# Induced attention and a leaky feed-forward net on one core: deferred softmax sums of the first group and a new order of the first 48 blocks

## The chip, the core and the metric

The kernel runs on one core of one Trainium2 chip. The metric is device time in microseconds (us) for one launch; before the change it is 1496.11 us, the median of 3 runs (1496.09 to 1496.35). Engines are called by the profile's names: PE (TensorE), DVE (VectorE), ACT (ScalarE), POOL (GpSimd), SP (SyncE, which here gives out nearly all DMA transfers).

## What is computed

`x` has 4 batches of 12480 tokens with 128 channels; `inducing` has 32 rows. First the 32 rows attend to all tokens of a batch (this gives `h`), then all tokens attend to `h`, then a feed-forward net with a leaky activation follows.

```python
def mab(q, kv):
    s = scale * (q @ kv.transpose(0, 2, 1))
    s = s - s.max(-1, keepdims=True)
    a = np.exp(s)
    a /= a.sum(-1, keepdims=True) + 1e-09
    return a @ kv
h = mab(I, x)
attn = mab(x, h)
g = np.maximum(0.01 * (attn @ w_in), attn @ w_in)
out = g @ w_out
```

## The kernel before, in words

The tokens of a batch are split into six groups of 2048 tokens (0 to 5) and a remainder of 192 (RG). A group makes four tiles of 512 tokens; there are 98 tiles. The net's inner width of 2048 is cut into 16 pieces of 128, so a tile is 16 blocks. A block (lines 697 to 760) is one product `ph` (L705: the second attention's weights times `h` times `w_in`, both in high and low halves), its positive part `ghi` on ACT (L718), the rest `glo` on DVE (L726) and three products into `po` (L744: `ghi` with `w_hi`, `glo` with `w_hi`, `ghi` with `w_lo`). The linear part of the activation is one more product per tile, with `m2s` (L763). `ph` has three buffers (`LOOK`), so that the product of block u+3 needs the `glo` of block u done. After a tile, DVE transposes `po` to `osb` (L773) and SP stores it in four transfers (L791).

Everything runs through two stages. Up to block 47 the program is written out in the table `ORDER`: each name is a step (function `start`, L822 on), and each engine gets its instructions in that order. Names used below: `W` warm-up products on PE; `T` and `C` transpose a piece of `x` (PE) and copy it; `S` scores, `M` their maxima, `X` and `N` their combination over partitions, `E` exponential, `Y` transpose, `Z` sum, `H` products with `x`, `K` their gathering; `z` and `rz` the sum over partitions and its inverse, `pre` and `K2` the last combination, `hT` the product that turns `h`; `a`, `b`, `o`, `t`, `p` convert a piece of the 64-bit weights (ACT, DVE, DVE, ACT, POOL: L1018 to L1044); `sh`, `sl` split a piece of `w_out` (ACT, POOL); `wt`, `wc`, `wm`, `wd` turn a piece of `w_in`, copy it, multiply it with `w_out` (`w_ps`, L1069) and add it up for `m2s`; `s2`, `y`, `ymx`, `ysub`, `yex`, `ysm`, `ysr`, `ymul`, `yT`, `ah`, `alo` are the second attention's scores and softmax of group 0 and the split of its weights; `rep` and `J` make from it the inputs `A` of tiles 0 and 1 (L1093, L1097), `dA` those of tiles 2 and 3 by transfers; the same names with a 1 are group 1, and `dB` spreads its `ahi` and `alo` into the inputs `A` of tiles 4 to 7, by 16 transfers (L656). `F`, `G`, `L`, `A`, `B` are `ph`, `ghi`, `glo`, the first `po` product and the other two of a block; `os` is a tile's transpose and store. Blocks 0 to 31 alternate between tiles 0 and 1.

From block 48 on a loop (at the end of the kernel function) gives out each block and, between blocks, steps of generators for the next batches, by a count of due work. `first_scores` loads the next batch's `x` in pieces `xc` with three buffers (L248, SP) that DVE transposes to `xT` (L395). The transposes stand in DVE's queue between `glo` of the running blocks. The order of this stage is fixed when the program is built.

```python
if u + LOOK < NT * NF:
    ffn_first(u + LOOK)
ffn_second(u)
```

Of the kernel before, what the change touches and what calls it, by code (L numbers as in the profile page):

```python
# [9 lines left out]
F32 = mybir.dt.float32  # L10
# [10 lines left out]
def induced_attention_then_leaky_ffn(  # L21
# [34 lines left out]
    while N - base >= 4 * TOK:  # L56
# [13 lines left out]
    LOADS = {17: 1, 24: 7}  # L70
    WEIGHTS = [("in", 0), ("out", 0), ("in", 1), ("out", 1), ("in", 2), ("out", 2), ("in", 3), ("out", 3)]
# [3 lines left out]
        W W W W W W W W indT T0.0 W T0.1 W T0.2 W W C0.1a T0.3 W W W C0.2v C0.3a C0.0a S0 T1.0 T1.1 C1.0v  # L75
        T1.2 C1.1a M0 C1.2a T2.0 T1.3 C2.0a T2.1 C1.3a T2.2 C2.1a C2.2v T2.3 S1 C2.3v S2 M1 T3.0 M2 T3.1
        T3.2 C3.0v C3.1a X0 C3.2a T3.3 N0 T4.1 E0 C3.3v T4.0 t0 S3 E2 E1 a0 b0 Y0 C4.1v H0 M3 T4.2 Y1 T4.3
        C4.0a o0 T5.0 C4.3a T5.2 C4.2v p0 C5.0a T5.1 Z1 C5.2a Y2 S4 C5.1a Z2 T5.3 a1 b1 M4 TR.0 t1 wt0 CR.0a
        o1 X1 C5.3a SR a2 b2 p1 N1 H1 MR E3 o2 S5 al1 t2 Z3 H2 a4 b4 p2 M5 wc0 W t4 K0 X2 o4 wt1 E4 wm0 N2
        p4 Y3 E5 Y4 H3 al2 a6 Z4 b6 t6 Z5 H4 o6 wd0 ER p6 wt2 a7 b7 Y5 ZR t7 K1 z o7 H5 wc1 rz p7 wc2 YR pre  # L80
        a5 HR wt3 K2 a3 hT b3 b5 hTc t3 o3 s2 wc3 o5 p3 sh3 hw y wm1 ymx wh t5 ysubv wl p5 yex wd1 hd0 ysm
        sg2 wm2 sh2 ysr sh0 ymulv sh1 s21 yT sl1 wd2 W ah wm3 alov sl0 hd1 rep0 wd3 y1 rep1 sl3 J0 ymx1 J1 F0 F1
        G0 m2 sgR ysub1g dA2 A0 L0 G1 F2 sl2 G2 B0 L1 mh F3 hd2 A1 L2 G3 B1 F4 L3 A2 G4 F5 B2 ml yex1 L4 A3 F6
        G5 B3 dA3 A4 L5 G6 F7 B4 G7 L6 F8 A5 B5 G8 L7 F9 A6 G9 B6 hd3 L8 F10 A7 ysm1 G10 B7 F11 L9 A8 G11 B8
        A9 L10 F12 B9 ysr1 G12 F13 L11 A10 ymul1g G13 B10 L12 A11 B11 A12 L13 F14 B12 G14 yT1 A13 F15 F16
        L14 G15 B13 A14 L15 G16 F17 B14 G17 A15 L16 B15 A16 L17 F18 B16 G18 A17 F19 L18 F20 G19 B17 A18 L19
        G20 B18 F21 A19 L20 G21 F22 B19 L21 G22 A20 F23 B20 G23 L22 A21 F24 B21 L23 G24 F25 A22 G25 B22 L24
        A23 B23 L25 F26 A24 G26 F27 B24 L26 G27 F28 A25 B25 G28 L27 A26 F29 B26 L28 G29 F30 A27 G30 B27 L29
        F31 L30 A28 G31 B28 os0 A29 F32 B29 L31 G32 F33 A30 L32 G33 B30 A31 F34 L33 B31 G34 A32 L34 ah1 F35
        B32 G35 alo1v A33 B33 L35 F36 dB F37 G36 A34 B34 L36 G37 F38 A35 B35 G38 L37 F39 A36 G39 B36 L38 A37  # L90
        F40 B37 L39 G40 A38 F41 L40 F42 G41 B38 A39 L41 G42 B39 F43 A40 L42 G43 B40 F44 os1 yg2 ygR A41 G44 B41 L43
        A42 F45 B42 L44 G45 A43 B43 L45 F46 A44 G46 B44 F47 L46 A45 G47 F48 B45 L47 G48 A46 F49 B46 G49 L48
        A47 F50 B47 L49 G50 L50 os2
# [25 lines left out]
    own = const.tile([P, 4], F32, tag="own", name="own")  # L119
    w_in_sb = const.tile([P, DFF], F32, tag="w_in_sb", name="w_in_sb")  # L120
# [573 lines left out]
    live, accs, fetches = {}, {}, []  # L694
    slots = [
# [72 lines left out]
    def store(t):  # L768
# [4 lines left out]
        nc.vector.transpose(osb[:, :n], po[:, :n])  # L773
        yield HEAVY
        o = 0
        for b, g, js in tiles[t]:
            base, J, K = GROUPS[g]
            n = 32 * K
            for j in js:
                row = b * N + base + j * 32 * K  # L780
                if len(tiles[t]) > 1:
                    dst = out[row : row + n, :].rearrange("(r k) c -> r k c", k=K)
                else:
                    dst = out[row : row + n, :].rearrange("(v r u) c -> r u v c", v=2, u=K // 2)
# [38 lines left out]
    def start(stacking, seconds, chosen):  # L823
# [57 lines left out]
        def peak(g):  # L881
            J, K, rows, w = size(g)
            p, i = step_of[g]
            if ("rd", p) not in V:
                V["rd", p] = small(f"rd{p}", 4 * len(STEPS[p]))
# [4 lines left out]
            rm = small(f"rm{g}")  # L890
            if J < 4:
# [5 lines left out]
            nc.vector.tensor_scalar(  # L897
                out=V["rd", p][:, 4 * i : 4 * i + 4], in0=own, scalar1=rm, scalar2=None, op0=ALU.mult,
                op1=ALU.min, accum_out=small("any"),
            )  # L900
            V["e", g] = e

        def X(p):
            n = 4 * len(STEPS[p])
            V["X", p] = pm = aux_ps("mx_ps")
            nc.tensor.matmul(pm[:, :n], same, V["rd", p], start=True, stop=True)
# [17 lines left out]
        def E(g):  # L924
            J, K, rows, w = size(g)
            V["zg", g] = zg = small(f"zg{g}")
            if J < 4:
# [16 lines left out]
        def Z(g):  # L944
            p, i = step_of[g]
            old, V["z"] = V["z"], small(f"z{g}")
            if i:
                nc.vector.tensor_tensor(out=V["z"], in0=old, in1=V["zg", g], op=ALU.add)
            else:
                nc.vector.tensor_scalar(  # L950
                    out=V["z"], in0=old, scalar1=V["al", p], scalar2=V["zg", g], op0=ALU.mult, op1=ALU.add
                )

# [46 lines left out]
        def pre():  # L1000
            p = len(STEPS) - 1
            V["pre"] = r = sb.tile([P, C], F32, tag="hacc", name="pre", bufs=2)
            nc.vector.tensor_scalar(
                out=r, in0=V["hacc", p - 1], scalar1=V["al", p], scalar2=V["rz"], op0=ALU.mult, op1=ALU.mult
            )
# [139 lines left out]
        def warm():  # L1145
# [7 lines left out]
            "W": warm, "z": z_product, "rz": rz, "pre": pre, "hT": hT_product, "hTc": hT_copy,  # L1153
# [7 lines left out]
        for i, end in enumerate(["", "1"]):  # L1161
# [3 lines left out]
            for name, n in [("ymx", 1), ("ysub", 1), ("yex", 2), ("ysm", 1), ("ysr", 1), ("ymul", 1), ("yT", 3)]:  # L1165
                plain[name + end] = lambda gen=gen, n=n: go(gen, n)
# [35 lines left out]
    with tc.manual_schedule():  # L1202
# [76 lines left out]
```

## Time and profile before

| what | value |
|---|---|
| median of 3 runs | 1496.11 us (1496.09 to 1496.35) |
| the profiled execution: its time, its span | 1496.72 us, 1494.6 us |
| PE busy | 1480.1 us (99%) |
| DVE, ACT, POOL busy | 1265.5 us (85%), 999.6 us (67%), 112.4 us (8%) |
| granted TensorE clock | 0.998 of full speed |
| HBM read, written | 48.94 MB, 25.56 MB |
| first `ph` product | 52.48 us after the span's start |

The profile shows one execution. The span runs from the first to the last instruction of the program; the time of the execution lies 2.1 us above it. Busy time of an engine is a union over its instructions; matmuls are pipelined, so that the start of one after another, and not the length of one, is PE's pace.

### The profile page before, as it was taken

The numbers are of one execution on the slowest core, as the hardware profiler recorded it, in microseconds if no ns is written. First come the engines' busy times: TensorE is split into PE (matmuls) and PEld (weight loads), VectorE is DVE, ScalarE is ACT, GpSimd is POOL, SyncE is SP. The second block draws the span as 40 slices with busy tenths as digits, with TensorE's granted clock in tenths as the row PEclk, the third lists the DMA queues.
The fourth block names the chain that finished last, engine by engine and source line by source line (L and its number), as shares of the span: only waits on it lengthen the run. The fifth ranks groups of instructions, "written<-read, shape, count | busy, mean of one in ns | idle before, by whom it ended". The sixth has DMA issues, their size and how long they took to land.

```text
span 1494.6 us, 22249 instructions
## 1 busy us (share of the span) xinstructions
PE 1480.1 (99%) x7861; PEld 1262.8 (84%) x7861; DVE 1265.5 (85%) x2137; ACT 999.6 (67%) x1748; POOL 112.4 (8%) x182
## 2 busy tenths in 40 slices
PE   8999999999999999999999999999999999999998
PEld 6788888888889888888888888888888898888887
DVE  6888898879898898789899898798888888888886
ACT  5766666666676666676676666676766766666665
POOL 1300100000100100000010100010100000000000
PEclk9999999999999999999999999999999999999999
DMA  8127446335444432243533531231212212212211
GB/s 285 44 56 137 82 78 158 61 59 95 82 103 82 111 82 50 43 96 69 110 69 68 135 67 19 43 73 20 50 34 38 43 25 49 43 24 48 41 26 22
DMA packets 402079, 105.23 MB, mean 70 GB/s; under 512 B 372624, under 2 KB 375088, under 8 KB 401968
## 3 DMA queue, kind: packets, MB, share of 16 engines
q1 hardware_dynamic: 401920, 103.80, 33.7%
q8 instruction: 62, 1.02, 0.3%
q14 instruction: 49, 0.40, 0.1%
q10 hardware_dynamic: 48, 0.02, 0.0%
HBM read 48.94 MB, written 25.56 MB: 50 GB/s over the span
## 4 chain that ended last, share of the span: by engine, by line
PE 95%; DMA 2%; DVE 1%; SPq 1%; ACT 0%; issue 0%; POOL 0%; DVEq 0%; ACTq 0%
PE po L744 67%; PE ph L705 23%; PE s_ps L262 3%; PE po L763 1%; PE h_ps L438 1%; DMA xr<-in_x_dram 1%; DMA raw<-in_moe_w_out_dram 0%; DMA raw<-in_moe_w_in_dram 0%; SPq L248 0%; SPq L833 0%; PE w_ps L1069 0%; DVE glo L726 0%; ACT ghi L718 0%; DMA xc<-in_x_dram 0%; PE hw_ps L545 0%
## 5 line engine op out<-in xcount | busy, mean ns | idle before, releaser
L718 ACT ACTIVATE ghi<-ph 128x512 fp32r<-128x512 f32 (+1 forms) x1568 | 929.5, 595 | 463.7 <-PE ph L705 458.5
L726 DVE SCALAR_TENSOR_TENSOR glo<-ph,ghi 128x512 fp32r<-128x512 f32 (+1 forms) x1568 | 1041.9, 679 | 185.4 <-ACT ghi L718 163.0
L705 PE MATMUL ph<-A,hws 128*128 128x512 f32 (+1 forms) x1600 | 596.6, 377 | 1.6 <-DVE glo L726 1.3
L744 PE MATMUL po<-ghi,w_hi 128*128 128x512 f32 (+1 forms) x1568 | 593.7, 379 | 0.0
L744 PE MATMUL po<-glo,w_hi 128*128 128x512 f32 (+1 forms) x1568 | 593.1, 378 | 0.0
L744 PE MATMUL po<-ghi,w_lo 128*128 128x512 f32 (+1 forms) x1568 | 593.0, 378 | 0.0
L705 PEld LDWEIGHTS ph<-A,hws 128*128 128x128 f32 x1600 | 301.9, 189 | 59.3 <-DVE glo L726 5.6
L744 PEld LDWEIGHTS po<-glo,w_hi 128*128 128x128 f32 x1568 | 296.4, 189 | 41.9 <-DVE glo L726 0.7
L744 PEld LDWEIGHTS po<-ghi,w_lo 128*128 128x128 f32 x1568 | 296.3, 189 | 41.1
L744 PEld LDWEIGHTS po<-ghi,w_hi 128*128 128x128 f32 x1568 | 296.4, 189 | 39.9 <-ACT ghi L718 0.2
L773 DVE STREAM_TRANSPOSE osb<-po 128x512 f32<-128x512 f32 (+1 forms) x98 | 68.8, 702 | 1.5 <-PE po L763 1.5
L644 POOL TENSOR_TENSOR alo<-aT,ahi 128x512 fp32r<-128x512 f32 x22 | 28.1, 1279 | 486.1 <-ACT ahi L639 451.4
L395 DVE STREAM_TRANSPOSE xT<-xc 128x512 f32<-128x512 f32 x72 | 50.5, 701 | 1.6 <-DMA xc<-in_x_dram 1.6
L597 POOL TENSOR_TENSOR y<-y,mx 128x512 f32<-128x512 f32 x23 | 24.2, 1051 | 278.5 <-DVE mx L595 218.7
L612 POOL TENSOR_TENSOR y<-y,sm 128x512 f32<-128x512 f32 x23 | 24.1, 1049 | 189.1 <-DVE sm L610 159.9
L763 PE MATMUL po<-A,m2s 128*128 128x512 f32 (+1 forms) x100 | 37.1, 374 | 0.0
L355 DVE STREAM_TRANSPOSE y<-s_ps 128x512 f32<-128x512 f32 x22 | 15.7, 715 | 10.8 <-PE s_ps L262 9.2
L262 PE MATMUL s_ps<-xT,indT 128*32 128x512 f32 x192 | 24.2, 595 | 0.5 <-ACT xT L871 0.5
L262 PE MATMUL s_ps<-xT,hT 128*32 128x512 f32 x192 | 24.0, 597 | 0.4 <-ACT hT L1013 0.4
L763 PEld LDWEIGHTS po<-A,m2s 128*128 128x128 f32 x100 | 18.9, 189 | 2.6
L280 DVE TENSOR_SCALAR_CACHE_REDUCE e<-s_ps 128x512 f32<-128x512 f32 x18 | 12.4, 690 | 8.3 <-PE s_ps L262 7.5
L438 PE MATMUL h_ps<-xr,ay 128*32 128x128 f32 x576 | 17.6, 274 | 0.0
(152 smaller groups left out, 376.6 us busy)
## 6 DMA issues: line engine op xcount, KB each, us to landing
xr<-in_x_dram SPq DMA_DIRECT2D x96, 256.0 KB, 5.1
out_dram<-osb SPq DMA_DIRECT2D x384, 64.0 KB, 2.2
xc<-in_x_dram SPq DMA_DIRECT2D x288, 64.0 KB, 2.7
A<-ahi SPq DMA_DIRECT2D x188, 64.0 KB, 2.0
A<-alo SPq DMA_DIRECT2D x188, 64.0 KB, 2.0
hws<-hilo SPq DMA_DIRECT2D x64, 64.0 KB, 2.0
raw<-in_moe_w_in_dram SPq DMA_DIRECT2D x4, 512.0 KB, 7.8
raw<-in_moe_w_out_dram SPq DMA_DIRECT2D x4, 512.0 KB, 8.3
```

The costliest lines, as they stand in the source:

```text
L262: nc.tensor.matmul(dst, lhsT, rhs, start=True, stop=True)
L395: nc.vector.transpose(t[:, j, :], blk.rearrange("p n c -> p (n c)"))
L438: nc.tensor.matmul(hp[32 * k : 32 * k + 32, :C], ay[:rows, 4 * q + k, :], xb[:rows, k, :], start=(i == 0 and q == 0), stop=(last[k] == i a ...
L597: engines[0].tensor_tensor(out=yv, in0=yv, in1=mx[:rows, :K].unsqueeze(2).broadcast_to([rows, K, M]), op=ALU.subtract,)
L612: engines[1].tensor_tensor(out=yv, in0=yv, in1=smv.unsqueeze(2).broadcast_to([rows, K, M]), op=ALU.mult)
L644: (engine or nc.gpsimd).tensor_tensor(out=alo[sl], in0=aT.pop((b, g))[: 32 * J, :], in1=ahi[sl].bitcast(F32), op=ALU.subtract,)
L705: nc.tensor.matmul(ph[:, o : o + w], hw[b][1][:, f * P : (f + 1) * P], woven(A4[t][:, o : o + w], t), start=True, stop=True,)
L718: nc.scalar.activation(halves(ghi[:, :n], t)[1], live[u][2], AF.Relu)
L726: nc.vector.scalar_tensor_tensor(out=halves(glo[:, :n], t)[1], in0=ph, scalar=0.0, in1=halves(ghi[:, :n], t)[1].bitcast(F32), op0=ALU.max, ...
L744: nc.tensor.matmul(accs[t][:, :n], w[:, f, :], woven(r[:, :n], t), start=(f == 0 and w is w_hi and r is live[u][0]), stop=False,)
L763: nc.tensor.matmul(accs[t][:, o : o + w], hw[b][2], woven(a4[:, o : o + w], t), start=False, stop=(o + w == n),)
L773: nc.vector.transpose(osb[:, :n], po[:, :n])
```

## The change

Four things change. (1) The second softmax of group 0 leaves its weights undivided: the sums and their inverse are made later, spread over partitions by a product (`sc`), copied (`sq`), and POOL multiplies the transposed output `osb` of tiles 0 to 3 with them before the store. The split reads the turned weights in another order of tokens, and the store of these tiles uses plain rows. (2) The last combination of `h` no longer takes the inverse sum: `pre` is gone, and ACT scales the matrix `same` of the product `hT` by it (`sr`). Maxima and sums of a step are combined once per step and not once per group. (3) The weights arrive in another order, all of `w_in` first, and the first of them after 21 pieces of `x` and not 18. (4) The table `ORDER` is new.

```diff
-    LOADS = {17: 1, 24: 7}
-    WEIGHTS = [("in", 0), ("out", 0), ("in", 1), ("out", 1), ("in", 2), ("out", 2), ("in", 3), ("out", 3)]
+    LOADS = {20: 1, 24: 7}
+    WEIGHTS = [("in", 0), ("in", 1), ("in", 2), ("in", 3), ("out", 0), ("out", 1), ("out", 2), ("out", 3)]
...
-        A42 F45 B42 L44 G45 A43 B43 L45 F46 A44 G46 B44 F47 L46 A45 G47 F48 B45 L47 G48 A46 F49 B46 G49 L48
-        A47 F50 B47 L49 G50 L50 os2
+        A45 B45 G47 L47 G48 A46 L48 F49 F50 G49 L49 G50 ymul1g os1 yT1 ah1 alo1v dB B46 A47 B47 os2 L50
+        ygR
...
         nc.vector.transpose(osb[:, :n], po[:, :n])
+        if t < 4:
+            turned = osb.rearrange("p (k c) -> p k c", c=32)
+            nc.gpsimd.tensor_tensor(
+                out=turned, in0=turned,
+                in1=token_scale[0][:, t, :].unsqueeze(2).broadcast_to([P, 16, 32]), op=ALU.mult,
+            )
...
         def X(p):
+            nc.vector.tensor_tensor(
+                out=rd.rearrange("p (n j) -> p n j", j=4),
+                in0=V["rm", p].unsqueeze(2).broadcast_to([P, n, 4]),
+                in1=own.unsqueeze(1).broadcast_to([P, n, 4]),
+                op=ALU.mult,
+            )
...
-                    out=new, in0=hp, scalar=V["rz"], in1=V["pre"], op0=ALU.mult, op1=ALU.add
+                    out=new, in0=V["hacc", p - 1], scalar=V["al", p], in1=hp, op0=ALU.mult, op1=ALU.add
...
-        def pre():
+        def scaled():
+            V["samez"] = r = sb.tile([P, P], F32, tag="samez", name="samez", bufs=1)
+            nc.scalar.mul(r, same, V["rz"])
...
-            nc.tensor.matmul(ph[:, :P], V["hs"], same, start=True, stop=True)
+            nc.tensor.matmul(ph[:, :P], V["hs"], V["samez"], start=True, stop=True)
...
+        def scales():
+            nc.vector.tensor_tensor(out=apart, ...
+            nc.tensor.matmul(
+                pc[:, :64], same, apart.rearrange("p t k -> p (t k)"), start=True, stop=True
+            )
+        def scales_copy():
+            nc.scalar.copy(r.rearrange("p t k -> p (t k)"), V.pop("sc")[:, :64])
...
         def split_high():
-            nc.scalar.copy(ahi, aT[0, 0])
+            nc.scalar.copy(ahi.rearrange("p (a b i) -> p a b i", a=2, b=16), turned_view(aT[0, 0]))
```

How the order moves, at three places.

PE between the copy of `hT` and the first blocks, before: after the scores of group 2 (`s_ps`) a `w_ps` group, the scores of group 1, and two more `w_ps` groups, the last behind warm-up products.

```order
L1069 MATMUL w_ps<-wraw,winT 128x128 x4
L262 MATMUL s_ps<-xT,hT 32x512 x4
L1148 LDWEIGHTS ident
L1148 MATMUL warm_ps<-ident 128x256
L1148 LDWEIGHTS ident
L1148 MATMUL warm_ps<-ident 128x256
L1069 MATMUL w_ps<-wraw,winT 128x128 x4
L1093 MATMUL a_ps<-ahi,pick 128x512
L1093 MATMUL a_ps<-alo,pick 128x512
L1093 MATMUL a_ps<-ahi,pick 128x512
L1093 MATMUL a_ps<-alo,pick 128x512
L705 MATMUL ph<-A_815,hws 128x512 x2
```

PE at the same place now, from the `a_ps` products on:

```order
L1162 MATMUL a_ps<-ahi,pick 128x512
L1162 MATMUL a_ps<-alo,pick 128x512
L1162 MATMUL a_ps<-ahi,pick 128x512
L1162 MATMUL a_ps<-alo,pick 128x512
L1217 LDWEIGHTS ident
L1217 MATMUL warm_ps<-ident 128x256
L1217 LDWEIGHTS ident
L1217 MATMUL warm_ps<-ident 128x256
L712 MATMUL ph<-A_727,hws 128x512 x3
L1085 MATMUL w_ps<-wraw,winT 128x128 x4
L751 MATMUL po<-ghi,w_hi 128x512
```

One `w_ps` group still stands before `a_ps`; three others, one turn of `w_in` and the product `sc_ps` now stand among the blocks.

DVE at the end of the 48 blocks, before: the transposes of the outputs of tiles 1 and 2 stand eight `glo` apart, and the split `alo` of group 1 twenty rows of work earlier.

```order
L773 STREAM_TRANSPOSE osb<-po 128x512
L726 SCALAR_TENSOR_TENSOR glo<-ph,ghi 128x512 x4
L644 TENSOR_TENSOR alo<-aT,ahi 128x512
L726 SCALAR_TENSOR_TENSOR glo<-ph,ghi 128x512 x8
L773 STREAM_TRANSPOSE osb<-po 128x512
L355 STREAM_TRANSPOSE y<-s_ps 128x512
L355 STREAM_TRANSPOSE yr<-m_ps 96x64
L726 SCALAR_TENSOR_TENSOR glo<-ph,ghi 128x512 x8
L773 STREAM_TRANSPOSE osb<-po 128x512
```

DVE at the same place now:

```order
L733 SCALAR_TENSOR_TENSOR glo<-ph,ghi 128x512 x16
L780 STREAM_TRANSPOSE osb<-po 128x512
L623 STREAM_TRANSPOSE aT<-y 128x512
L646 TENSOR_TENSOR alo<-aT,ahi 128x512
L780 STREAM_TRANSPOSE osb<-po 128x512
L733 SCALAR_TENSOR_TENSOR glo<-ph,ghi 128x512
L357 STREAM_TRANSPOSE yr<-m_ps 96x64
```

The transpose of tile 1's output, the weights' transpose, the split and the transpose of tile 2's output now stand together between the 50th `glo` and the 51st.

SP before, from the store of tile 0 to the first `xc` loads of the next batch (the spread `dB` is 16 transfers to four tiles `A4`, the first two are shown, and the last):

```order
L791 DMA out_0_dram<-osb_1137 256x2x32 x4
L656 DMA A4_1192<-ahi_1175 32x512
L656 DMA A4_1192<-alo_1176 32x512
...
L656 DMA A4_1207<-alo_1176 32x512
L791 DMA out_0_dram<-osb_1279 256x2x32 x4
L791 DMA out_0_dram<-osb_1353 256x2x32 x4
L248 DMA xc_1408<-in_x_dram 32x2x32 x12
L248 DMA xc_1421<-in_x_dram 32x16x32 x8
```

SP at the same place now:

```order
L804 DMA out_0_dram<-osb_1122 512x1x32 x4
L804 DMA out_0_dram<-osb_1297 512x1x32 x4
L658 DMA A4_1310<-ahi_1306 32x512
L658 DMA A4_1310<-alo_1307 32x512
...
L658 DMA A4_1325<-alo_1307 32x512
L804 DMA out_0_dram<-osb_1336 512x1x32 x4
L250 DMA xc_1396<-in_x_dram 32x2x32 x12
L250 DMA xc_1409<-in_x_dram 32x16x32 x8
```

The store of tile 1 now stands ahead of the spread of group 1's weights, which waits for the split at the end of DVE's rows above; the `xc` loads stand behind both. From block 48 on the rows of all engines are the same as before, apart from the form of the stores of tiles 1 to 3 and POOL's multiplications.

## Rows read from the trace of the kernel before

**Rows 1.** Page, part 4: the chain that ended last, share of the span by engine.
```profile
PE 95%; DMA 2%; DVE 1%; SPq 1%; ACT 0%; issue 0%; POOL 0%; DVEq 0%; ACTq 0%
```

**Rows 2.** Timeline of PE near block 49 (start us, us, engine line op out<-in).
```profile
94.82 0.38 PE L705 MATMUL ph<-A,hws 128*128 128x512 f32 x1
...
98.27 0.38 PE L705 MATMUL ph<-A,hws 128*128 128x512 f32 x1
```

**Rows 3.** Chain in the first 60 us, in order of time (start us, us, what).
```profile
34.23 0.95 PE winT_ps L1059 x4
...
35.18 1.71 PE w_ps L1069 x8
...
40.49 1.20 DVE pre L1003
...
42.72 0.27 ACT hT L1013
...
52.48 0.70 PE ph L705 x2
```

**Rows 4.** Timelines of DVE and PE, 132 to 139 us: their waits.
```profile
137.44 0.71 DVE L395 STREAM_TRANSPOSE xT<-xc 128x512 f32<-128x512 f32 x1 [1.60 <-DMA xc<-in_x_dram]
...
138.78 0.48 PE L705 MATMUL ph<-A,hws 128*128 128x512 f32 x1 [1.06 <-DVE glo L726]
```

**Rows 5.** Groups of the first 100 us by form (count | busy us, mean ns).
```profile
L773 DVE STREAM_TRANSPOSE osb<-po 128x512 f32<-128x512 f32 x3 | 2.1, 705 | 0.0
...
L644 DVE TENSOR_TENSOR alo<-aT,ahi 128x512 fp32r<-128x512 f32 x1 | 0.7, 683 | 0.0
...
L639 ACT CAST ahi<-aT 128x512 fp32r<-128x512 f32 x1 | 0.6, 617 | 0.0
```

**Rows 6.** Tile raw in the first 60 us (duration ns min/median/max).
```profile
L1022 DVE TENSOR_SCALAR cv_b<-raw x8: 415/420/1521, 20.7 to 42.4; 128x512 int32<-128x512 int32 x8
```

**Rows 7.** Timeline 36.5 to 60 us: a weight turn and a weight product on PE.
```profile
40.92 0.66 PE L1059 MATMUL winT_ps<-ident,w_in_sb 128*128 128x128 f32 x4
...
45.20 1.16 PE L1069 MATMUL w_ps<-wraw,winT 128*128 128x128 f32 x8 [0.24 <-POOL wraw L1044]
```

**Rows 8.** Timeline 36.5 to 60 us: one block from ph to glo.
```profile
54.91 0.38 PE L705 MATMUL ph<-A,hws 128*128 128x512 f32 x1
...
55.33 0.60 ACT L718 ACTIVATE ghi<-ph 128x512 fp32r<-128x512 f32 x1 [0.17 <-PE ph L705]
...
55.95 0.69 DVE L726 SCALAR_TENSOR_TENSOR glo<-ph,ghi 128x512 fp32r<-128x512 f32 x1 [0.25 <-ACT ghi L718]
```

**Rows 9.** Timeline of SP, 58 to 190 us: transfers given out, by name.
```profile
83.11 0.56 SPq L656 DMA_DIRECT2D A<-ahi  x1
...
93.82 6.87 SPq L791 DMA_DIRECT2D out_dram<-osb  x8
...
100.73 19.27 SPq L248 DMA_DIRECT2D xc<-in_x_dram  x28
...
120.04 3.46 SPq L220 DMA_DIRECT2D xr<-in_x_dram  x7
...
123.60 2.74 SPq L791 DMA_DIRECT2D out_dram<-osb  x4
...
126.38 1.82 SPq L220 DMA_DIRECT2D xr<-in_x_dram  x2
...
128.30 13.03 SPq L248 DMA_DIRECT2D xc<-in_x_dram  x16
```

**Rows 10.** Chain in the first 200 us: a transfer from issue to landing.
```profile
134.67 2.58 DMA xc<-in_x_dram
```

**Rows 11.** Timelines to 60 us: POOL operations, and glo beside one.
```profile
31.28 1.27 POOL L1044 TENSOR_TENSOR w_in_sb<-cv_a,cv_t 128x512 int32<-128x512 int32 x1 [0.70 <-ACT cv_t L1034]
...
53.59 1.05 POOL L597 TENSOR_TENSOR y<-y,mx 128x512 f32<-128x512 f32 x1
...
53.63 2.08 DVE L726 SCALAR_TENSOR_TENSOR glo<-ph,ghi 128x512 fp32r<-128x512 f32 x3 [0.82 <-ACT ghi L718]
```

More of the change, by code (lines that the diff above doesn't have):

```diff
@@ L694, in induced_attention_then_leaky_ffn, with plain_rows @@
     live, accs, fetches = {}, {}, []
+    token_scale = []
+    def plain_rows(t):
+        return t < 4 or len(tiles[t]) > 1
     slots = [
@@ L883, in peak @@
             p, i = step_of[g]
-            if ("rd", p) not in V:
-                V["rd", p] = small(f"rd{p}", 4 * len(STEPS[p]))
+            n = len(STEPS[p])
+            if ("rm", p) not in V:
+                V["rm", p] = small(f"rm{p}", n)
             if g == RG:
@@ L896, in peak @@
             )
[L897 to L900, printed above, removed]
             V["e", g] = e
         def X(p):
-            n = 4 * len(STEPS[p])
+            n = len(STEPS[p])
+            rd = small(f"rd{p}", 4 * n)
+            nc.vector.tensor_tensor(
[4 more added lines that the diff above has]
+            )
             V["X", p] = pm = aux_ps("mx_ps")
-            nc.tensor.matmul(pm[:, :n], same, V["rd", p], start=True, stop=True)
+            nc.tensor.matmul(pm[:, : 4 * n], same, rd, start=True, stop=True)
         def least(p):
@@ L925, in E @@
             J, K, rows, w = size(g)
-            V["zg", g] = zg = small(f"zg{g}")
+            p, i = step_of[g]
+            if ("zg", p) not in V:
+                V["zg", p] = small(f"zg{p}", len(STEPS[p]))
+            zg = V["zg", p][:, i : i + 1]
             if J < 4:
@@ L942, in Y, with Z @@
             )
[L944 to L949, printed above, removed]
+        def Z(p):
+            z = small(f"zs{p}")
+            nc.vector.tensor_reduce(out=z, in_=V["zg", p], op=ALU.add, axis=AX.X)
+            if p:
+                new = small(f"z{p}")
                 nc.vector.tensor_scalar(
-                    out=V["z"], in0=old, scalar1=V["al", p], scalar2=V["zg", g], op0=ALU.mult, op1=ALU.add
+                    out=new, in0=V["z"], scalar1=V["al", p], scalar2=z, op0=ALU.mult, op1=ALU.add
                 )
+                z = new
+            V["z"] = z
         def H(g):
@@ L1080, in w_add, with first_second @@
                 )
+        def first_second():
+            y = early.pop((0, 0))
+            mx = sb.tile([P, 16], F32, tag="mx", name="mx")
+            nc.vector.tensor_reduce(out=mx, in_=y, op=ALU.max, axis=AX.X)
+            yield
+            chosen["ysub"].tensor_tensor(
+                out=y, in0=y, in1=mx.unsqueeze(2).broadcast_to([P, 16, M]), op=ALU.subtract
+            )
+            yield
+            nc.scalar.activation(y, y, AF.Exp, scale=SCALE)
+            V["y"] = y
+            yield
@@ new lines, in first_turned, with first_sums, first_inverse @@
+        def first_turned():
+            t = sb.tile([P, TOK], F32, tag="aT", name="aT", bufs=4)
+            nc.vector.transpose(t, V["y"].rearrange("p k m -> p (k m)"))
+            aT[0, 0] = t
+        def first_sums():
+            V["sm"] = sm = sb.tile([P, 16], F32, tag="sm", name="sm")
+            nc.vector.tensor_reduce(out=sm, in_=V.pop("y"), op=ALU.add, axis=AX.X)
+        def first_inverse():
+            nc.vector.tensor_scalar_add(V["sm"], V["sm"], 1e-9)
+            nc.vector.reciprocal(V["sm"], V["sm"])
@@ new lines, in scales @@
+        def scales():
+            apart = sb.tile([P, 4, 16], F32, tag="apart", name="apart", bufs=1)
+            nc.vector.tensor_tensor(
+                out=apart,
+                in0=V.pop("sm").unsqueeze(1).broadcast_to([P, 4, 16]),
+                in1=own1.unsqueeze(2).broadcast_to([P, 4, 16]),
+                op=ALU.mult,
+            )
+            V["sc"] = pc = aux_ps("sc_ps")
+            nc.tensor.matmul(
+                pc[:, :64], same, apart.rearrange("p t k -> p (t k)"), start=True, stop=True
+            )
@@ L1086, in split_low @@
         def split_low(engine):
             V["alo"] = alo = sb.tile([P, TOK], F32R, tag="alo", name="alo", bufs=1)
-            engine.tensor_tensor(out=alo, in0=aT.pop((0, 0)), in1=V["ahi"].bitcast(F32), op=ALU.subtract)
+            four = "p (a b i) -> p a b i"
+            engine.tensor_tensor(
+                out=alo.rearrange(four, a=2, b=16),
+                in0=turned_view(aT.pop((0, 0))),
+                in1=V["ahi"].bitcast(F32).rearrange(four, a=2, b=16),
+                op=ALU.subtract,
+            )
@@ L1152, in start @@
         plain = {
-            "W": warm, "z": z_product, "rz": rz, "pre": pre, "hT": hT_product, "hTc": hT_copy,
+            "W": warm, "z": z_product, "rz": rz, "sr": scaled, "sc": scales, "sq": scales_copy, "hT": hT_product, "hTc": hT_copy,
             "m2": m2_product, "mh": m2_high, "ml": m2_low,
```

75 lines of the change are left out of this document (39 added, 36 removed).

## Prediction

> **What bounds the kernel now.** I read the chain that ended last first: 95% of the span is TensorE [rows 1]. So the time is the moment at which TensorE's unbroken stream of blocks begins, plus the work left to it, plus whatever stops it afterwards. A block is one `ph` product and three `po` products at a steady pitch of 0.216 us, 0.864 us a block: from 94.82 to 98.27 there are four blocks and the one product with `m2s` of tile 2 [rows 2]. Then I read the chain of the start up to the first `ph` at 52.48 [rows 3], and last the queue of SP behind the 48 woven blocks, because the one later stop of TensorE is there: DVE waits 1.60 us for a transfer `xc` and TensorE loses 1.06 us of it [rows 4].
>
> **The start, up to the first block.** What the title names is worth almost nothing by itself: without the sums, their inverse and the multiplication the softmax is some 2 us shorter (two full-tile operations at about 0.7 us [rows 5] and two small ones), but TensorE, in its fixed order, was busy with `w_ps` and `s_ps` until the `a_ps` products began. The order has to bring the gain.
> Before `hT` three things leave the chain: the turn and the product of the weights between `mx` and `h_ps` (0.95 + 1.71 us), and `pre` (1.20 us), whose place the scaling of `same` on ACT takes beside other work [rows 3]. The third is a sign extraction `cv_b` ahead of the last maximum, which took 1.52 us where the median is 0.42 [rows 6]; I count 1.10. Sum 4.96, say 5.0. If the stretched `cv_b` only moves, 3.9 remain; if two more conversions of some 0.7 us leave with it, 6.4.
> After `hT` TensorE sets the pace in both orders. Before: three `s_ps` groups, `hw_ps`, three `w_ps` at 1.16, warm-up and `a_ps`. Now: the same with one `w_ps` and two turns at 0.66 [rows 7]. That is 2 × 1.16 − 2 × 0.66 = 1.0 us less. The softmax, 2 us shorter, now ends before these products do.
> So the first `ph` comes **6.0 us earlier** (bounds 4 and 8.5), near 46.5.
>
> **What moves behind the first block.** Three `w_ps` groups (3.5 us), one turn (0.66) and the new product of the scales (64 columns, less than half a turn, 0.26) stood before the stream or nowhere; now they stand in it, and a stream that never idles pays each in full: **+4.4 us** (3.9 if gaps between them overlap, 4.9 with gaps). Four conversions on DVE, the late sum and the scales go there too. DVE then has 50 `glo` at 0.69 us [rows 11], 34 us, and some ten other full-tile operations at 0.7 [rows 5] with small ones between: about 44 us in a stretch of 47. I take **+1.0 us** of stops (bounds −0.9, the stops before has there, and +3). The scaling of the outputs on POOL (four times about 1.05 us) lies beside TensorE and delays only stores.
>
> **The end of the woven blocks.** On DVE the transpose of tile 1's output, the transpose of the weights and the split `alo` of the next four tiles now follow the 50th `glo` directly, with the transpose of tile 2's output behind them, and only then the 51st `glo`. Time counted from the product `ph` of block 49: its `glo` ends at 1.73 [rows 8]; output transpose to 2.4, weights' transpose to 3.0, `ahi` on ACT to 3.65, `alo` to 4.4 [rows 5], tile 2's transpose to 5.1, the 51st `glo` to 5.7. The product of block 53 needs the buffer that this `glo` frees (three `ph` buffers). TensorE would be there at 3.45 [rows 2]: **+2.3 us** (bounds 1.5 if DVE runs ahead, 3.3 if `alo` stretches beside POOL as one `cv_b` did [rows 6, 11]).
>
> **The queue of SP.** This decides. Before, the 16 transfers of the spread of the next four tiles go out from 83.11, tile 1's and tile 2's stores up to 100.69, and the `xc` loads from 100.73 on, without a break; SP gives out one 64 KB transfer per 0.63 to 0.81 us, and that is what makes the fifth block of `xc` late [rows 9]. Its last transfer is issued at 134.67 and lands 2.58 us later [rows 10]; from the first spread transfer to this landing it is 137.25 − 83.11 = 54.1 us. Now the spread can start only after `alo` and behind tile 1's store, whose data POOL multiplies first: `glo` 1.73, transpose to 2.4, POOL to 3.5 (1.05 us for such an operation [rows 11]), store issues 2.7, so 6.2 after the product of block 49. Tile 1's store (half of 6.87 us) is already out, so 50.7 us follow and the load lands at 56.9. DVE wants it, without a wait, 37.6 us after block 53's product (135.84 − 98.27 [rows 2, 4]), which is now at 5.7: at 43.3. The wait is 13.6 us instead of 1.60. DVE stands in order, with the `glo` of the next blocks behind the transpose, and TensorE waits for them. Earlier `xc` loads, which came in time before, are late as well and take parts of the same sum. Of 1.60 us TensorE lost 1.06, a cushion of 0.54; with it used once, 13.6 − 0.54 − 1.06 = 12.0 more, with it used at two waits 11.5. I take **+11.5 us**; the lower bound is 8.3 (the 60 issues of that stretch at the spread's own 0.66 in place of their mean of 0.71), the upper 12.5.
>
> **A rule against the trace.** A `cv_b` that usually takes 0.42 us took 1.52 beside a POOL operation [rows 6, 11]; three `glo` beside another POOL operation took 2.08 us, their usual pitch [rows 11]. The Trainium skill, SBUF — State Buffer, section "SBUF: two separate sides", says that a DVE operation with two SBUF inputs or in a 2-port mode and a GpSimd operation shut each other out for a whole instruction; `glo` has one SBUF input, and the rows agree. By that rule `alo`, with two, could wait out the new POOL multiplication of tile 1's output beside it; the sum would then be 14.2 instead of 13.2.
>
> **The sum.** −6.0 + 4.4 + 1.0 + 2.3 + 11.5 = **+13.2 us** on the profiled execution, whose own time is 1496.72 (span 1494.6 and 2.1 around it); it lies 0.61 above the median 1496.11, so I forecast **1509.3 us** against the median. Not all ends meet; about ±4.5 covers this case: 1504.8 to 1513.8.
>
> **Rivals.**
> *SP keeps up (not slower).* The place is the same queue, the price the whole 11.5 us. It decides at the pace: between the first spread transfer and the late load there are 60 transfers of 64 KB or less and nine of the rows at 5.3 us together; 6.2 + 60p + 5.3 + 2.6 = 43.3 gives p = 0.49 us. Below that nothing is late. For it: the nine `xr` loads, four times as large, go out at 0.5 to 0.9 us [rows 9]. Against it: whole groups at 0.63 to 0.81 without a pause [rows 9]. Then the sum is +1.7: 1497.8, within what can be told from no change; with the start's best bounds (−8.5 + 3.9 − 0.9 + 1.5 = −4.0) 1492.1, faster. Chance 0.12.
> *DVE becomes the bound of the woven part.* If conversions beside POOL stretch to 1.5 us as one did and `glo` comes late throughout, the stops there cost 3 to 6 us rather than 1.0: about 1513. For it: 44 of 47 us busy. Against it: the median of the eight `cv_b` beside the same POOL work is still the short one [rows 6]. Chance 0.08.
> *The start gives nothing.* The loads end at the same time and the conversions of all four input pieces must precede `hw_ps`; if the fourth is late by as much as the order gains, the start's 6.0 is 1 to 2: 1513.8. Chance 0.05.
> The forecast keeps 0.75.
>
> **How the numbers follow.** A difference of 0.2%, 3 us, is about what a measurement tells from no change. Faster: a third of the first rival and a little for what I have not seen, 0.06. Same: the other two thirds, 0.08. Slower: 0.86. The range, 1502 to 1514, takes the forecast's own, both slower rivals, and part of the way to the first; it leaves out that one and the outer tails, less than 2 in 10.
>
> **What would show it.** First `ph` near 46.5 (44 to 48.5); `hT` copied near 38; three `w_ps` inside the stream. TensorE's first stop of about 2 us at block 53, ended by `glo`. The spread transfers begin some 6 us after block 49's product, the `xc` loads some 20 us after it; DVE then waits for `xc` several times, 12 to 14 us in all, TensorE idles 10 to 12 us, all before 160. From there on the two traces run alike. I am wrong in the main point if DVE waits for `xc` under 5 us in all; wrong in the start if the first `ph` is later than 49 or earlier than 43.

## The result and the profile after

The changed kernel takes **1507.27 us**, the median of 4 runs (1505.13 to 1508.68), against 1496.1 us for the kernel before on the same chip: a ratio of 1.0078, with a 95% interval of 1.0066 to 1.0090. The change makes the kernel slower by 11 us. The forecast was 1509.3 in a range of 1502 to 1514.

Three moments divide the two profiled executions: the first `ph` product, the `ph` product of block 53 (the first one given out by the loop), and the first scores `s_ps` of the loop that use `hT`.

| stretch | before | after | difference | predicted |
|---|---|---|---|---|
| start to first `ph` | 52.48 | 45.05 | -7.43 | -6.0 |
| first `ph` to block 53's | 45.79 | 51.49 | +5.70 | +7.7 (4.4 + 1.0 + 2.3) |
| block 53's `ph` to `s_ps` | 53.88 | 65.87 | +11.99 | +11.5 |
| `s_ps` to the end of the span | 1342.45 | 1342.69 | +0.24 | 0 |
| span | 1494.6 | 1505.1 | +10.5 | +13.2 |

The page's chain answers to [rows 1]: TensorE still makes nearly all of it.

```profile
PE 94%; DMA 2%; SPq 1%; DVE 1%; ACT 1%; issue 0%; DVEq 0%; ACTq 0%
```

**The start.** The chain in order of time, from the copy of `hT` to the first `ph` (start us, us, what), to be held against [rows 3]:

```profile
36.78 0.27 ACT hT L1029
...
37.10 1.92 PE s_ps L264 x16
39.03 1.22 PE hw_ps L547 x8
...
40.33 0.61 ACT hilo L554
40.96 0.68 DVE hilo L556
...
41.68 0.72 DVE aT L1113
42.43 0.68 ACT ahi L1147
43.13 0.70 DVE alo L1152
...
43.88 0.97 PE a_ps L1162 x3
44.84 0.23 PE warm_ps L1217 x2
45.08 0.95 PE ph L712 x3
```

`hT` is copied 5.94 us earlier, and from there to the first `ph` it is 8.27 us in place of 9.76. Behind `hT`, from 40.33 to 43.83, five operations on ACT and DVE (the split of `hws`, the turn and the split of the first group's weights) ended last. But TensorE was busy beside them with turns, `s_ps` and `w_ps`, and came only 0.1 us too early for `alo`. Its timeline:

```profile
43.31 0.47 PE L1162 MATMUL a_ps<-ahi,pick 128*128 128x512 f32 x1
43.88 0.50 PE L1162 MATMUL a_ps<-alo,pick 128*128 128x512 f32 x1
```

In the kernel before TensorE had three waits in this stretch: 0.24 us for POOL [rows 7], 0.30 for POOL again, and 0.22 for ACT ahead of the first `ph`, 0.76 in all. The second of them:

```profile
47.66 1.16 PE L1069 MATMUL w_ps<-wraw,winT 128*128 128x128 f32 x8 [0.30 <-POOL wraw L1044]
```

**The end of the woven blocks.** TensorE's timeline (start us, us, engine line op out<-in xcount, in brackets the idle time before and what ended it):

```profile
93.37 0.45 PE L751 MATMUL po<-ghi,w_hi 128*128 128x512 f32 x1 [0.40 <-DVE osb L780]
...
96.54 0.45 PE L712 MATMUL ph<-A,hws 128*128 128x512 f32 x1 [1.42 <-DVE yr L357]
```

Idle time is counted from the modelled end of a product, 0.38 us behind its start, and products start every 0.216 us. By the pace of the starts the two stops cost more than the 1.82 in brackets: block 53's product comes 5.68 us behind block 49's (90.86), where it was 3.45 before, so 2.23.

**The queue of SP**, its timeline, against [rows 9]: the spread of group 1 (`A`) begins at 97.09 in place of 83.11, and the loads `xc` at 111.38 in place of 100.73.

```profile
77.82 19.14 SPq L804 DMA_DIRECT2D out_dram<-osb  x8
97.09 0.55 SPq L658 DMA_DIRECT2D A<-ahi  x1
...
108.04 0.59 SPq L658 DMA_DIRECT2D A<-alo  x1
108.73 2.61 SPq L804 DMA_DIRECT2D out_dram<-osb  x4
111.38 18.31 SPq L250 DMA_DIRECT2D xc<-in_x_dram  x28
...
139.10 10.66 SPq L250 DMA_DIRECT2D xc<-in_x_dram  x16
```

What DVE and then TensorE make of it, where [rows 4] had one wait of 1.60 us and one stop of 1.06. DVE's timeline:

```profile
120.42 0.38 DVE L391 STREAM_TRANSPOSE xTr<-xc 128x192 f32<-128x192 f32 x1 [4.46 <-DMA xc<-in_x_dram]
...
126.31 0.71 DVE L397 STREAM_TRANSPOSE xT<-xc 128x512 f32<-128x512 f32 x1 [3.73 <-DMA xc<-in_x_dram]
...
146.02 0.71 DVE L397 STREAM_TRANSPOSE xT<-xc 128x512 f32<-128x512 f32 x1 [4.23 <-DMA xc<-in_x_dram]
```

TensorE's timeline:

```profile
121.43 0.79 PE L712 MATMUL ph<-A,hws 128*128 128x512 f32 x1 [3.60 <-DVE glo L733]
122.02 0.63 PE L751 MATMUL po<-ghi,w_hi 128*128 128x512 f32 x1
122.44 0.63 PE L751 MATMUL po<-glo,w_hi 128*128 128x512 f32 x1
...
127.65 0.48 PE L712 MATMUL ph<-A,hws 128*128 128x512 f32 x1 [0.73 <-DVE glo L733]
...
147.36 0.63 PE L712 MATMUL ph<-A,hws 128*128 128x512 f32 x1 [3.69 <-DVE glo L733]
...
149.50 0.63 PE L712 MATMUL ph<-A,hws 128*128 128x512 f32 x1
...
151.10 0.38 PE L712 MATMUL ph<-A,hws 128*128 128x512 f32 x1
```

DVE waits 12.42 us for `xc`, TensorE stops for 8.02. Look also at the pitch: behind the stop at 121.43 the products follow each other at 0.42 to 0.43 us, twice the 0.216 of before. Busy time by windows (us, PE busy, PEld, DVE, ACT, POOL, PEclk, DMA share, GB/s) has it as the granted clock:

```profile
90.00:100.00 10.00, 8.18 (x37) 6.40 (x36) 8.15 (x15) 5.33 (x10) 3.15 (x3) 1.00 0.27 48
100.00:110.00 10.00, 10.00 (x48) 8.77 (x47) 8.79 (x16) 7.27 (x13) 1.05 (x1) 1.00 0.37 87
110.00:120.00 10.00, 7.84 (x37) 6.52 (x35) 5.38 (x9) 5.43 (x10) 1.35 (x2) 1.00 0.24 36
120.00:130.00 10.00, 7.84 (x23) 5.94 (x24) 5.84 (x11) 3.23 (x7) 0.00 (x0) 0.66 0.59 92
130.00:140.00 10.00, 10.00 (x48) 8.77 (x47) 9.35 (x18) 6.86 (x12) 0.29 (x1) 1.00 0.87 220
140.00:150.00 10.00, 6.31 (x25) 4.97 (x24) 5.01 (x9) 3.71 (x7) 0.78 (x1) 0.88 0.77 132
```

After two stops of 3.6 us TensorE runs at its lower level, 1.2 GHz, for some blocks. The 11.99 us are then 6.96 of more stops (8.02 less 1.06), 2.90 for the blocks from 121.43 to 127.65 (6.22 us, less the wait of 0.73, less three blocks at 0.864), 1.80 for the two blocks and the `m2s` product behind the third stop (3.74 against 1.94), and 0.3 of small gaps at the restarts.

### The profile page after: what moved, and what is told of

Read it like the earlier page. It is cut to its first block, busy times and chain, and to the rows that moved or that the text cites. A ratio compares the mean times of both kernels' runs of the same rounds, so it can differ in the third digit from the quotient of the medians.

```text
span 1505.1 us, 22252 instructions
## 1 busy us (share of the span) xinstructions
PE 1484.8 (99%) x7863; PEld 1264.3 (84%) x7863; DVE 1265.1 (84%) x2128; ACT 997.6 (66%) x1746; POOL 116.9 (8%) x186
## 4 chain that ended last, share of the span: by engine, by line
PE 94%; DMA 2%; SPq 1%; DVE 1%; ACT 1%; issue 0%; DVEq 0%; ACTq 0%
PE po L751 66%; PE ph L712 22%; PE s_ps L264 2%; PE po L770 1%; DMA xr<-in_x_dram 1%; PE h_ps L440 1%; SPq L250 1%; DMA xc<-in_x_dram 0%; DVE glo L733 0%; PE hw_ps L547 0%; ACT ghi L725 0%; PE h_ps L985 0%; PE w_ps L1085 0%; SPq L658 0%; DVE osb L780 0%
## 5 line engine op out<-in xcount | busy, mean ns | idle before, releaser
L282 DVE TENSOR_SCALAR_CACHE_REDUCE e<-s_ps 128x512 f32<-128x512 f32 x18 | 12.4, 691 | 8.3 <-PE s_ps L264 7.5
```

## The experiments

The theory: **the place of the late spread in SP's queue** makes the `xc` loads late. The rivals: the arithmetic that the title names (POOL's multiplications, plain rows, late sums), tile 1's store, and the amount of data itself. Each ratio is taken to runs of the kernel before on the same chip; their medians were 1495.59 us for experiments 1 to 4, 1496.47 for 5 to 8 and 1497.28 for 9.

**1. The changed kernel with an early spread.** `ysm1` and `ysr1` stood behind `A29` and `L33`; the rest of the table stays.

```diff
+L25 ysm1 yex1
...
+L27 ysr1 ymul1g L28
...
+L31 yT1 F33
...
+B32 ah1 A33 G34 L34 alo1v dB F36
...
+L42 L43 os1 F45
...
-G50 ymul1g os1 yT1 ah1 alo1v dB B46
+G50 B46
```

> The changed kernel with the second group's softmax, its split, the 16 spread transfers and tile 1's store put earlier among the woven blocks (the spread behind L34 in place of behind L50); all else as changed. Theory (the late spread pushes the xc loads back in SP's queue): 1492.6 us, 1491 to 1495, under the kernel before, because the start's 7.4 us stay and the queue's 12 us go; block 53's product near 94.7 without a stop over 0.5 us ahead of it, DVE waits for xc 1 to 2.5 us in all where the changed kernel has 12.4, and TensorE's granted clock stays at full speed from 110 to 160. Rival (the multiplications on POOL, the plain-row stores or a fuller DVE make the loads late): 1503 or more, and waits for xc above 8 us.

Measured 1495.39 us (1492.86 to 1497.66, 11 runs), ratio to before 0.9997 (0.9988 to 1.0006). The loss of 11 us is gone, so the rival falls. In its profiled run (1492.86) the first `ph` of the loop comes at 94.97, and SP and DVE read:

```profile
97.94 19.08 SPq L251 DMA_DIRECT2D xc<-in_x_dram  x28
```

```profile
133.68 0.71 DVE L398 STREAM_TRANSPOSE xT<-xc 128x512 f32<-128x512 f32 x1 [1.03 <-DMA xc<-in_x_dram]
```

DVE's one wait is in the range expected, and the loop's first `ph` is near the 94.7 named. But part of that is luck: in this execution the first `ph` of all came at 43.95, 1.1 us earlier than in the changed kernel, and TensorE had a stop among the blocks where none over 0.5 us was expected:

```profile
72.37 0.48 PE L713 MATMUL ph<-A,hws 128*128 128x512 f32 x1 [0.79 <-DVE glo L734]
```

The median is 2.8 us above what I expected, and only the profiled run is near it. What the other runs lose there no trace shows; experiment 7 bears on it.

**2. The kernel before with a late spread.** Nothing else is changed.

```diff
-L34 ah1 F35 B32 G35 alo1v A33 B33 L35 F36 dB F37
+L34 F35 B32 G35 A33 B33 L35 F36 F37
...
+L46 ah1 A45 G47 F48 B45 L47 alo1v G48
...
+B47 dB L49 G50 L50 os2
```

> The kernel before with one thing alone: the split of the second group's weights and the 16 spread transfers moved from behind L34 to B47 behind L50's neighbours, so that on SP's queue they follow tile 1's store. Theory (place of the spread in SP's queue): 1504.6 us, 1502 to 1507, DVE waits for xc about 10 us in all, and after stops of TensorE longer than 3 us its granted clock falls to half for some blocks. Rival (the other parts of the change make the loads late): stays at 1496, one wait of about 1.6 us.

Measured 1505.97 us (5 runs), ratio 1.0065 (1.0052 to 1.0077): three moved steps in the old kernel make a loss of 10 us. The start, 7 us shorter in the changed kernel, is as long as before here. From block 53's product to `s_ps` they cost 9.41 us of the 11.99. SP's queue and TensorE's stops:

```profile
94.38 0.56 SPq L658 DMA_DIRECT2D A<-ahi  x1
...
109.48 18.34 SPq L250 DMA_DIRECT2D xc<-in_x_dram  x28
```

```profile
125.20 0.48 PE L707 MATMUL ph<-A,hws 128*128 128x512 f32 x1 [2.72 <-DVE glo L728]
...
146.48 0.79 PE L707 MATMUL ph<-A,hws 128*128 128x512 f32 x1 [5.25 <-DVE glo L728]
```

DVE's waits for `xc` are 9.7 us in all. The blocks behind the stop of 2.72 us keep the full clock; those behind 5.25 run at half.

**3. The changed kernel with tile 1's store earlier.** `os1` stands behind `L43`.

```diff
+L42 L43 os1 F45
...
-G50 ymul1g os1 yT1 ah1
+G50 ymul1g yT1 ah1
```

> The changed kernel with only the output transpose, multiplication and store of tile 1 moved from behind the 50th glo to behind L43. Theory (the late spread is what counts, tile 1's store ahead of it only adds its own length): 1504.5 us, 1503 to 1506; the spread starts near 95 in place of 97.1, the 0.4 us stop behind it and half of block 53's stop go, the waits for xc fall by 1.5 to 2.5 us of 12.4. Rival (tile 1's store, with its multiplication on POOL, is the cause): below 1498.

Measured 1505.45 us (5 runs), ratio 1.0057 (1.0045 to 1.0070): the theory's value, not the rival's. The spread starts at 94.90, and the waits for `xc` are 10.0 us. The stop of 0.40 is gone; the one at block 53 stays whole (1.5 us), so that half of this expectation failed.

**4. The arithmetic alone,** on the order, the loads and the first blocks of before (parts 1 and 2 of the change, with `ysm`, `ysr`, `sc`, `sq` behind the first blocks as in the change).

```diff
-rz p7 wc2 YR pre a5
+rz sr p7 wc2 YR a5
...
-yex wd1 hd0 ysm sg2 wm2 sh2 ysr sh0 ymulv sh1 s21 yT
+yex wd1 hd0 sg2 wm2 sh2 sh0 sh1 s21 yT
```

> The kernel before, with its order, its order of loads and its first blocks, but with the change's arithmetic: sums of the first group kept off its weights, outputs of the first four tiles multiplied by the inverse sums on POOL, inverse sum in the matrix of the hT product, maxima and sums taken once per step. Theory (what the title names is worth almost nothing by itself, the order makes the result): 1495.1 to 1496.5 us, within 0.2% of before; first ph at 50.5 to 52.5, spread from 83 on as before, one wait for xc of 1 to 2 us. Rival (the multiplications on POOL and the plain-row stores delay what follows): 1498 or more; second rival (the shorter softmax shortens the start by its 2 us): below 1494.5.

Measured 1497.28 us (11 runs), ratio 1.0007 (0.9998 to 1.0016): no change within 0.2%, 0.8 us above the range that I gave, and neither rival. The first `ph` comes at 50.96, 1.52 us earlier. All of this lies ahead of `hT`, where `pre` is gone; the shorter softmax gives nothing, for from `hT` to the first `ph` it is 9.75 us (before: 9.76).

```profile
41.21 0.24 ACT L1030 COPY hT<-hT_ps 128x128 f32<-128x128 f32 x1
```

`s_ps` comes at 152.42, 0.27 later than before: a stop of 0.65 us ahead of the scales' product and a longer wait for `xc` (2.35 us) take the gain back.

**5. The spread issued by GpSimd.**

```diff
-                        nc.sync.dma_start(
+                        (nc.gpsimd if engine else nc.sync).dma_start(
```

> The changed kernel with the 16 late spread transfers issued by GpSimd in place of SP; order, amount and place of everything else as changed. Theory (what is late is the issue on SP's one queue): the xc loads start near 100 in place of 111.4, the waits of DVE for xc fall from 12.4 to 1.5 to 4 us, no half clock after 110; 1496.5 us, 1495 to 1498.5. Rival (the amount of data through the shared DMA engines makes the loads late, whoever issues them): waits above 9 us and 1504 or more.

Measured 1503.19 us (5 runs), ratio 1.0041 (1.0029 to 1.0054): between the two. The waits for `xc` fall from 12.4 to 2.5 us with the same transfers, and the loads start 10.42 us behind block 53's product in place of 14.84. So the amount of data is not the cause; in the changed kernel the DMA engines were busy for only 0.24 to 0.37 of the time from 90 to 120. Not all of the fall is the loads' doing, for DVE comes later too, held up by the stop shown below. The Trainium skill, "DMA: Bandwidth & Descriptors", section "Issuing engines are not separate DMA queues", says that issuing from several engines saves only the issue time, for all share the same DMA engines. The trace agrees: the loads start 4.4 us earlier, and issue time is what was short here. A new wait stands in place of the old. GpSimd's timeline, then TensorE's:

```profile
101.75 0.50 POOL L658 DMA_DIRECT2D A<-alo  x1
102.27 1.06 POOL L783 TENSOR_TENSOR osb<-osb,scr 128x512 f32<-128x512 f32 x1
103.27 1.05 POOL L599 TENSOR_TENSOR y<-y,mx 128x512 f32<-128x512 f32 x1
```

```profile
106.25 0.51 PE L712 MATMUL ph<-A,hws 128*128 128x512 f32 x1 [3.88 <-DVE glo L733]
```

The 16 issues hold GpSimd from 94.20 on, and its next operation starts at 102.27. Tile 2's multiplication stands behind them, hence its store and the `xc` loads behind it (106.38, where I expected 100); so does the subtraction of the next softmax, ACT waits for that with its exponential (4.59 us), `ghi` waits behind the exponential, and TensorE stops for 3.88 us up to 106.25. Half clock follows this stop and, where I expected none after 110, a later one of 1.96 us.

**6. TensorE kept busy in its stops.**

```diff
+            if u in (74, 77, 95):
+                keep_busy()
```

Each call is 32 products of the identity with 256 columns, into a tile that nothing reads.

> The changed kernel with 32 products of 256 columns (3.4 us, written to a PSUM tile that nothing reads) ahead of each of the three first products that wait for the late loads, so that TensorE works through its long stops. Theory (the half clock after the stops of 3.6 us and more comes of the stops, and its cost is the part that no wait hides): granted clock 1.00 from 110 to 160, two blocks behind the third stop at 0.864 us a block, so 1.8 us earlier from there on: 1505.5 us, 1504 to 1507. Rival (the clock falls for another reason): still half after the stops, 1507 or more.

Measured 1506.70 us (4 runs), ratio 1.0071 (1.0057 to 1.0084): undecided. The profile shows the slowest of the four. Both first stops are filled and the clock there stays at 1.00, but TensorE only arrives earlier at the third wait, now 6.4 us on DVE; 2.34 us of it stay open, and behind them the clock falls.

**7. The early spread, with the stores of tiles 0 to 2 issued by GpSimd.**

```diff
-                    nc.sync.dma_start(dst[..., 32 * cb : 32 * cb + 32], src)
+                    (nc.gpsimd if t < 3 else nc.sync).dma_start(dst[..., 32 * cb : 32 * cb + 32], src)
```

> The kernel with the early spread (expected and run before: 1495.4 us median, but 1492.9 in the profiled run, whose one wait for xc was 1.0 us), with the stores of tiles 0 to 2 issued by GpSimd, which has just multiplied them, in place of SP. Theory (what keeps that kernel from its 1492.6 is how little time the xc loads have left): xc loads start near 91 in place of 97.9, no wait for xc, 1492 us, 1490.5 to 1493.5. Rival (the spread of the run times has nothing to do with the loads, it comes from the start): 1494 to 1496 with the wait for xc gone. Rival (GpSimd's own issues delay its multiplications or DVE beside them): 1497 or more.

Measured **1493.65 us** (1492.92 to 1494.81, 11 runs), ratio to before 0.9980 (0.9971 to 0.9989): faster than both kernels. SP gives out the `xc` loads from here on:

```profile
91.06 18.79 SPq L251 DMA_DIRECT2D xc<-in_x_dram  x28
```

DVE does not wait for `xc`, and TensorE does not stop between 95 and 160 us. The median lies 1.7 us above the one forecast and 1.7 us below that of experiment 1, which ran on another chip, with a profiled span that is 0.9 us longer than there. The runs lie closer together (1.9 us against 4.8). That fits the theory that the other runs of experiment 1 lost their time to late loads; with one trace of each it is not shown.

**8. The order alone:** the change's `ORDER` and loads on the arithmetic of before, with `pre` behind `rz`, `ysm ysr ymulv` behind `yex`, the sums `Z` by group and no `sc` and `sq`.

```diff
-rz a4 wt1 t3 K2 sr hT
+rz pre a4 wt1 t3 K2 hT
...
-s21 yex wc0 wm0 yT
+s21 yex ysm ysr ymulv wc0 wm0 yT
```

> The kernel before with the change's order of the first 48 blocks and order of loads, but with the arithmetic of before: the first group's weights divided by their sums ahead of the first block, stores and sums as before. Theory (the order makes the result, the arithmetic next to nothing): 1508 us, 1506 to 1510; first ph 1 to 2 us later than in the changed kernel's 45.05 because the softmax is longer by two operations, DVE waits for xc 11 to 14 us. Rival (the multiplications of the outputs on GpSimd carry a share of the loss): below 1503.

Measured 1509.39 us (4 runs), ratio 1.0083 (1.0067 to 1.0098). The order alone makes the loss; the waits for `xc` are 10.6 us, a little under the 11 expected. The first `ph` is 2.96 us later than in the changed kernel, more than the 1 to 2 that I expected. The chain has `hT`, then the first `ph`; TensorE's timeline has its wait between them:

```profile
37.78 0.27 ACT hT L1015
...
48.01 0.97 PE L707 MATMUL ph<-A,hws 128*128 128x512 f32 x3
```

```profile
46.12 0.51 PE L1095 MATMUL a_ps<-ahi,pick 128*128 128x512 f32 x1 [1.48 <-ACT ahi L1086]
```

One microsecond of it lies ahead of `hT`, a moment that is not the same in every execution: in seven traces with the new order, its loads and the new arithmetic the copy of `hT` starts between 35.69 and 37.54. From there to the first `ph` these seven take 8.26 to 8.28 us and this kernel 10.23. So in the new order the shorter softmax is worth 1.96 us, in the range that I expected.

**9. As 6, with 60 products ahead of the third block.**

```diff
-                keep_busy()
+                keep_busy(60 if u == 95 else 32)
```

> The changed kernel with the products that nothing reads ahead of the three waiting blocks, as in the run with 32 each, but 60 (6.4 us) ahead of the third, since the first two fills removed the half clock there and only let TensorE arrive earlier at the third wait, of which 2.3 us stayed uncovered. Theory (the half clock follows the stop): granted clock 1.00 to 160, the block that waits third near 150 as with 32, the two behind it at 0.864 us a block, 1.8 us earlier than with 32 from there on: 1505 us, 1503.5 to 1506.5. Rival (the clock falls there whatever TensorE does): two blocks at 1.7 us again, 1506.5 or more.

Measured 1508.44 us (5 runs), ratio 1.0077 (1.0063 to 1.0091). The clock stays at 1.00 to 160, and the blocks behind the third wait run at full pace:

```profile
149.55 0.46 PE L712 MATMUL ph<-A,hws 128*128 128x512 f32 x1
150.50 0.38 PE L770 MATMUL po<-A,m2s 128*128 128x512 f32 x1
150.71 0.38 PE L712 MATMUL ph<-A,hws 128*128 128x512 f32 x1
151.58 0.38 PE L712 MATMUL ph<-A,hws 128*128 128x512 f32 x1
```

The two blocks take 2.03 us against 3.74, so the half clock follows the stops and its price is 1.71. The time did not fall: `xc` was transposed at 146.09, from which the changed kernel needed 1.34 us more to its block, but the products ran on to 149.55. I had made them 2.1 us too long, which cost more than the clock gave back.

**All runs side by side.** In each kernel, the time from block 53's `ph` to the first `xc` issue, and to `s_ps`:

| kernel | first `xc` | `s_ps` |
|---|---|---|
| 7 early spread, stores by GpSimd | -4.79 | 53.17 |
| before | 2.46 | 53.88 |
| 1 early spread | 2.97 | 53.41 |
| 4 arithmetic alone | 3.55 | 54.62 |
| 5 spread by GpSimd (with its own stop) | 10.42 | 62.49 |
| 2 before, late spread | 10.82 | 63.29 |
| 3 store earlier | 12.56 | 64.17 |
| 8 order alone | 13.59 | 66.64 |
| 6 filling products, 32 | 14.34 | 68.00 |
| 9 filling products, 60 at the third wait | 14.78 | 67.10 |
| after | 14.84 | 65.87 |

Up to about 3 us little is lost. Beyond experiment 4 a microsecond of delay costs about one of time, not on a clean line: 2, 3, 8 and after have 7.3 to 11.3 us more delay than 4 and lose 8.7 to 12.0 us more. Experiments 5, 6 and 9 have losses of their own.

## Why the prediction was right

**The queue of SP (+11.5, measured +11.99): the mechanism is right, and shown** by experiments 2 and 1, which bring the loss into the old kernel and take it out of the new, and by 8, where the order alone makes it. The waits of DVE are 12.4 us, within the 12 to 14 named beforehand. TensorE idles for 8.0 us there and not the 10 to 12 named: 6.96 are stops beyond those of before, and 4.7 are blocks at half clock, of which the prediction has no word.

That the sum came within 0.5 us is in part luck. The late block was worked out to reach DVE 12.0 us later, counted from block 53's product; its transpose began 49.48 us behind that product in place of 39.17, so 10.3 later, since the transfers up to it went out 2.1 us faster than in the kernel before, where a single `xc` issue took 3.0 us (130.96). From that transpose to `s_ps` it then took 1.7 us more than before, and the half clock behind the third stop costs about that much (1.71 in experiment 9). The 2.90 us ahead of the second wait cost nothing by themselves: at full clock, in experiment 9, that stretch of three blocks took 6.54 us (120.67 to 127.21) against 6.22, since the transfers set its end.

**The end (+2.3, measured +2.23): right.** Block 53's product came 5.68 us behind block 49's, as worked out (5.7), and 3.45 was the pace without stops. That pace is 16 products, the one with `m2s` among them; the prediction's four blocks and one product would be 17. The stop ends with `yr`, which stands behind the 51st `glo`, not with that `glo`.

**The woven stops (+1.0, measured none) and the moved work (+4.4, measured 3.47): mis-sized.** The feared stops among the first blocks don't exist in the changed kernel; DVE's load there was no bound, and that rival fell. What is left of 5.70 without the 2.23 is the moved work. The three `w_ps` groups took 1.09, 0.89 and 0.89 us of the chain, the turn 0.44 and the scales 0.17; I had taken 1.16, 0.66 and 0.26, from the start's rows.

**The start (-6.0, measured -7.43): mis-sized, 0.9 us of it ahead of `hT` and 0.5 behind.** Ahead of `hT` 5.94 us were gained where 5.0 were worked out. Which of the three terms gave more is not shown, and since the copy of `hT` moves by up to 1.9 us between executions of this start, part of the 0.9 may be chance. Behind `hT` 1.49 were gained where 1.0 was worked out: "After `hT` TensorE sets the pace in both orders" holds but for TensorE's own waits, 0.76 us before ([rows 7] shows the first of them) and 0.09 now. By that 0.09 the softmax does not end before the products. What was said of it in the old order came true: in experiment 4 it gives nothing behind `hT`, and the kernel's time is the same within 0.2%. In the new order TensorE waits 1.48 us for `ahi` without it, and it is worth 1.96 us at the first block (experiment 8).

**The rule on DVE and GpSimd** did not come to bear: `alo` began at 94.50 and took 0.69, when POOL's multiplication (93.30, 1.05 us) was over. But `pre`, whose 1.20 us [rows 3] the prediction took as its price, was stretched like the `cv_b`: a POOL operation ran beside it (40.32 to 41.60), and in experiment 8, with none beside it, `pre` took 0.35. The rival "SP keeps up" fell: the 16 spread transfers alone took 0.73 us each (97.09 to 108.73), where it needed 0.49. "The start gives nothing" fell with the first `ph` at 45.05.

So the sum was 2.7 us too high: 1.4 from the start and 2.0 from the woven blocks and their end, less 0.5 for the queue and 0.2 behind it.

## What to carry to other kernels

Where one queue gives out stores, spreads and prefetches in program order, a step that is moved back moves every later transfer on that queue, and those may be waited for 20 to 50 us later; read the queue's timeline from the moved step to the next wait before judging a new order. The time that the start gains is worth nothing until the transfers keep up; with the spread back in its place and the stores on the engine that had just finished them, the changed arithmetic and the early start are worth 0.2% (experiment 7: of 7.75 us gained at the first block, the woven blocks take 5.33 back). An engine that is given a queue's issues pays for them in its own work, so count what stands behind them.

## What was not expected of the hardware

TensorE's granted clock fell from 2.4 to 1.2 GHz for some two to three blocks after stops, which the kernel before, with its one stop of 1.06 us, never shows in this stretch. All six stops of 3.56 us and more, in five kernels, were followed by it. Of the shorter ones some were (1.96 us in experiment 5, 2.77 in experiment 8, 2.34 in experiment 6, there after its filling products) and some not (2.46 in experiment 8, 2.69 in experiment 3, 2.72 in experiment 2). The Trainium skill, "TensorE: Matmul & The Clock Gate", section "HAM oscillation — how this bites in real kernels", describes waits for DMA that send TensorE to half clock; the trace agrees. Experiments 6 and 9 show that work which fills the wait prevents it. GpSimd gave out a 64 KB transfer in 0.50 us, SP the same spread in 0.73 us a transfer, and on GpSimd its own operations stood behind them.
